# Spreading the reciprocals of later chunks by 32-row matmuls in a four-layer attention and MLP kernel

## The chip, the cores and the metric

The kernel runs on one core of a Trainium2 chip. The metric is the device time of one execution in microseconds. A core has five engines with a queue each: TensorE (PE) multiplies matrices, VectorE (DVE), ScalarE (ACT) and GpSimd (POOL) work element by element, and SyncE (SP) starts most DMAs. Matmuls write to PSUM, which has eight banks of 512 f32 columns by 128 partitions; ACT and DVE read them from there.

## The reference

The input is 2048 rows of 576 bf16 values. Four layers follow each other: attention (A), MLP (B), and both again with the same weights. The two layers, cut to what matters:

```python
def A(x):                       # x is already layer-normalized; 32 heads of 18
    q, k, v = split(x @ wqkv)
    pq, pk = phi(q), phi(k)     # phi(t) = (t + 1 if t > 0 else exp(t)) + 1e-6
    kv = einsum("bhsd,bhse->bhde", pk, v)
    z = einsum("bhsd->bhd", pk)
    num = einsum("bhqd,bhde->bhqe", pq, kv)
    den = einsum("bhqd,bhd->bhq", pq, z) + 1e-6
    return (num / den[..., None]) @ wo
def B(x):                       # x is layer-normalized, and once more in here
    return gelu(layernorm(x) @ w1 + b1) @ w2 + b2
x = x + A(layernorm(x)); x = x + B(layernorm(x))    # twice
```

## The kernel before

Rows are held in 16 blocks of 128 tokens; four blocks make a chunk of 512. The 32 heads lie in five groups (g): four of seven heads (126 rows) and one of four heads (72 rows). PE's instructions stand in the order in which the code writes them (each is chained to the one before). On the other engines a scheduler orders the instructions, and the code adds edges ("after=...") that keep one behind another on the same engine; such an edge is an order and no wait.

An attention layer first computes keys, values and most query maps, sums keys by values (kvT), and multiplies that into the output weights (kv_wo, L733; kvwo is its result). Then, by chunk:

- q_proj (L584) makes a query map of a group: five matmuls of 512 columns into a bank of ps_h, then phi by ACT (exp, L466, and identity, L467) and DVE (min and max) into pq. Some are left for this part of the layer: in layer 0 the last three, in layer 2 the last one; they are taken in the loop over blocks.
- den_stage (L748): 20 matmuls, with the array split into four tiles of 32 columns, give the denominators of a chunk as a 128 x 128 tile: partition 32j + h holds head h, and the columns are the tokens of block j. ACT takes the reciprocal by a logarithm and an exp (rden, one buffer).
- quad_stage (L767): DVE lays rden out as 128 x 512, zero outside its own quarter (quad_rden).
- scale_stage (L777): for a group, one matmul of 512 columns with a 0/1 matrix (head_bc) spreads the reciprocals over the rows of the group's heads; ACT copies the bank to SBUF (rden_bc), and DVE multiplies pq by it.
- wo_stage (L789): for a block, ten matmuls (five groups, two halves) accumulate the output in accA or accB in turn; DVE adds the residual row (L517), and SP stores the sum.

PSUM has two pools: ps_h, four banks of one kind that all of q_proj, den_stage, scale_stage and the transposes share, and accA and accB, of two banks each, for outputs, kv_wo and the few tiles written with a pair tag.

The entry (L802 to L829) does the steps of chunk 0 and the denominators of chunk 1. The loop over blocks (L830 to L849) then runs wo_stage for block t, takes a query map if one is left, and spreads the next chunk's reciprocals in its first two blocks, for three groups and then two; den_stage of the chunk after that follows in the second.

The sums of blocks 0 to 3 are also normalized for the MLP. LNPipe (L301) moves each through steps, one per tick: statistics (DVE by bn_stats, L351, or ACT by two passes with an accumulator, L333 and L342), the inverse root, the norm on POOL (L391), five transposes on PE (L423) and a copy by ACT. hold is the number of ticks before the statistics; the loop gives two ticks for each block up to 9, and one for the others. tp_at is the block behind which the transposes may go. In layer 0 the sums go to row buffers of a pool of nine, which a block keeps until it is normalized and stored; in layer 2 they overwrite the residual's own buffer.

The tile `turned` holds rows that DVE transposes for later chunks in the MLP layers.

Of the kernel before, what the change touches and what calls it, by code (L numbers as in the profile page):

```python
# [15 lines left out]
P = 128  # L16
# [12 lines left out]
CA = 512  # L29
# [5 lines left out]
def build(tc, A_x, A_wqkv, A_wo, B_w1, B_b1, B_w2, B_b2, out, dbg=None, n_layers=4):  # L35
    nc = tc.nc
    dbg = dbg or {}
    with ExitStack() as ctx:
# [420 lines left out]

        def phi_from_psum(ps_ap, out_ap, rows, n, turned_cols=False, after=None, dve_after=None, ident_after=None):  # L460
            e = work.tile([P, 512], BF16, name="phi_e", bufs=3)
            a = work.tile([P, 512], BF16, name="phi_a", bufs=2)
            e_out, a_out = e[0:rows, 0:n], a[0:rows, 0:n]
            if turned_cols:
                e_out, a_out, ps_ap = spread(e_out), spread(a_out), gather(ps_ap)
            exp = nc.scalar.activation(out=e_out, in_=ps_ap, func=ACT.Exp)  # L466
            ident_pass = nc.scalar.activation(out=a_out, in_=ps_ap, func=ACT.Identity, bias=C1, scale=1.0)  # L467
            if after is not None:
                for step in (exp, ident_pass):
                    tc.add_manual_dep(step.ins, after, NOSYNC, reason="broadcasts first")  # L470
            if ident_after is not None:
                tc.add_manual_dep(ident_pass.ins, ident_after, NOSYNC, reason="first rows first")
# [54 lines left out]
        def layer_A(li, next_kind, pre_a1=None):  # L527
# [56 lines left out]
            def q_proj(g, c, defer=False):  # L584
# [6 lines left out]
                if g == 0:  # L591
                    nc.gpsimd.memset(pq[(g, c)][96:P, 0:CA], 1.0)
                phi = lambda after=None, dve_after=None: phi_from_psum(qp[0:GR[g], :], pq[(g, c)][0:GR[g], 0:CA], GR[g], CA,
                                                       turned_cols=(li > 0), after=after, dve_after=dve_after)
                if defer:
# [137 lines left out]
            def kv_wo(g):  # L733
# [5 lines left out]
                out = kvwo[g][0:GR[g], :].rearrange("p (h n) -> p h n", h=2)  # L739
                if g % 2 or g == 4:  # L740
                    nc.vector.tensor_copy(out=out, in_=wp[0:GR[g], :, 0:HALF])
# [3 lines left out]
            quad_rden = {}  # L745
            rden_of = {}

            def den_stage(c, after=None, pair=None):  # L748
# [16 lines left out]
                rden_of[c] = rden  # L765

            def quad_stage(c, after=None):  # L767
# [8 lines left out]

            def scale_stage(g, c, pair=None):  # L777
                if pair:
                    bp = ps_acc.tile([P, 2, 512], F32, name="rden_pair", tag=pair)[:, 0, :]
                else:  # L780
                    bp = ps_h.tile([P, 512], F32, name="rden_ps", tag="h")
                pe(nc.tensor.matmul(bp[:, 0:CA], lhsT=head_bc[:, g, :], rhs=quad_rden[c][:, 0:CA], start=True, stop=True))  # L782
                rb = blk.tile([P, D], BF16, name="rden_bc", tag="blk")
                act_last["copy"] = nc.scalar.copy(out=rb[0:GR[g], 0:CA], in_=bp[0:GR[g], :]).ins.name
                mult = nc.vector.tensor_tensor(out=pq[(g, c)][0:GR[g], 0:CA], in0=pq[(g, c)][0:GR[g], 0:CA],  # L785
                                               in1=rb[0:GR[g], 0:CA], op=ALU.mult)
                dve_last["mult"] = mult.ins.name

            def wo_stage(t):  # L789
# [8 lines left out]
                if xn is not None and next_kind == "B" and t < TPC:  # L798
                    lnp.feed(xn, t, "B", "pool", "act", hold=(2, 4, 6, 8)[t], tp_at=6 + 2 * t,
                             **(dict(after="sum") if t % 2 else dict(stats="act", after="rden")))  # L800

# [9 lines left out]
            quad_stage(0)  # L811
            phi(after=act_last["rden"], dve_after=dve_last["quad"])
            if li > 0:
# [10 lines left out]
            late.append(q_proj(*q_left.pop(0), defer=True))  # L824
            scale_stage(4, 0)
            den_stage(1, after=act_last["copy"], pair="accB")
# [3 lines left out]
            for t in range(NT):  # L830
# [256 lines left out]
```

## Time and profile before

| | |
|---|---|
| Median of 3 runs | 766.45 us (766.34 to 767.07) |
| Profiled execution | 767.19 us, of which the span from first to last instruction 765.4 |
| Granted TensorE clock | 1.00 throughout |
| PE, busy | 759.5 us, 6522 matmuls |
| ACT, DVE, POOL, busy | 336.9, 271.8, 123.4 us |
| Layer 0, entry (70.7 to 77.7 us) | PE 6.81 of 7.00 us busy |
| Layer 0, loop over blocks (77.7 to 107.0) | PE 28.78 of 29.30, ACT 21.38, DVE 22.91 |
| Layer 2, entry (447.9 to 453.8) | PE 5.90 of 5.90 |
| Layer 2, loop over blocks (453.8 to 480.4) | PE 26.46 of 26.60, ACT 19.29, DVE 22.06 |

Times in the profile are microseconds from the first instruction. PEld is the loading of matmul weights, which runs beside the matmuls. A row of the timeline merges instructions of one line that follow each other, and where its engine sat idle before it, it names the releaser. Busy PE time counts overlapping matmuls as one stretch, with ends that are modelled, so a wait of PE is best read from the starts of successive rows.

### The profile page before, as it was taken

To read this page: it belongs to the slowest core of one execution; us is meant where nothing else is said; L and a number is where in the kernel's file an instruction comes from. 1 tells how busy PE (TensorE), PEld (TensorE's weight loads), DVE (VectorE), ACT (ScalarE), POOL (GpSimd) and SP (SyncE) were. 2 spreads that over 40 slices of the span, in tenths; PEclk is the share of its full clock that TensorE was granted. 3 is DMA by queue.
4 is the path that set the end of the run, shared out by engine and by line. 5 is a ranking of instruction groups with operands and counts; after the bars stand their busy time and mean duration, and the time that the engine had idled before them with its cause. 6 is when DMAs were issued, how large, how long until landed. Compare 5 with 4: busy or idle time off the path is not lost.

```text
span 765.4 us, 15654 instructions
## 1 busy us (share of the span) xinstructions
PE 759.5 (99%) x6522; PEld 492.3 (64%) x6522; DVE 271.8 (36%) x685; ACT 336.9 (44%) x752; POOL 123.4 (16%) x198
## 2 busy tenths in 40 slices
PE   8999999999999999999999999999999999999998
PEld 5776664675477457646777767447745764674476
DVE  7786864035113603400455678600240032000000
ACT  5888856304710660174057577560065036205600
POOL 4681322012100301200110004200020021001000
DMA  9992483016401631330246007530141033011000
GB/s 259 269 301 48 140 283 75 25 57 166 121 24 63 188 76 40 95 88 1 66 128 216 1 16 233 218 81 17 56 110 42 16 125 81 9 32 55 2 9 24
DMA packets 80289, 73.82 MB, mean 96 GB/s; under 512 B 36698, under 2 KB 64858, under 8 KB 80218
## 3 DMA queue, kind: packets, MB, share of 16 engines
q1 hardware_dynamic: 80218, 72.82, 32.4%
q8 instruction: 51, 0.84, 0.5%
q14 instruction: 20, 0.16, 0.1%
HBM read 48.03 MB, written 24.77 MB: 95 GB/s over the span
## 4 chain that ended last, share of the span: by engine, by line
PE 97%; ACT 1%; DVE 1%; DMA 1%; POOL 0%; issue 0%; SPq 0%; DVEq 0%
PE m_ps L968 36%; PE h_ps L910 20%; PE hp_ps L910 16%; PE q_ps L587 5%; PE wo_ps L794 4%; PE k_ps L539 3%; PE k_ps L610 3%; PE k_ps L627 2%; PE v_ps L560 1%; PE m_half L968 1%; PE v_ps L557 1%; PE tp L423 1%; PE rden_ps L782 1%; DMA wqkv_sb<-in_A_wqkv_dram 1%; PE kvacc L581 1%; PE k_tail L627 1%
## 5 line engine op out<-in xcount | busy, mean ns | idle before, releaser
L968 PE MATMUL m_ps<-w_sb,hT 128*128 128x288 bf16 x2232 | 274.8, 286 | 0.0
L968 PEld LDWEIGHTS <-hT 128*128 128x128 bf16 x2304 | 224.8, 98 | 59.8 <-issue 3.4
L910 PEld LDWEIGHTS <-w_sb 64*128 64x128 bf16 x2304 | 124.5, 94 | 136.5 <-issue 1.9
L910 PE MATMUL hp_ps<-yT,w_sb 64*128 64x512 bf16 x1152 | 178.0, 376 | 0.0
L910 PE MATMUL h_ps<-yT,w_sb 64*128 64x512 bf16 x1152 | 148.0, 376 | 0.0
L915 ACT COPY relay_sb<-relay_sb 128x1 f32<-128x1 f32 x144 | 28.6, 198 | 262.3 <-PE h_ps L910 220.0
L906 ACT ACTIVATE hT<-h_ps,b1T 128x512 bf16<-128x512 f32 x144 | 91.2, 684 | 44.4 <-PE h_ps L910 43.7
L374 POOL TENSOR_TENSOR ln_rstd<-ln_u,neg_half 128x1 f32<-128x1 f32 x64 | 36.7, 575 | 375.0 <-DVE ln_u L365 226.8
L906 ACT ACTIVATE hT<-hp_ps,b1T 128x512 bf16<-128x512 f32 x144 | 91.2, 693 | 0.0
L517 DVE TENSOR_TENSOR xbf<-m_ps,xo 128x576 bf16<-128x576 f32 x15 | 11.4, 758 | 212.8 <-PE m_ps L968 212.8
L517 DVE TENSOR_TENSOR xo<-m_ps,xo 128x576 f32<-128x576 f32 x16 | 12.1, 758 | 174.5 <-PE m_ps L968 174.5
L500 POOL TENSOR_TENSOR xo<-xo,b_bc 128x576 f32<-128x576 f32 x32 | 40.9, 1282 | 98.8 <-DMA xo<-x_d 59.8
L910 PE MATMUL h_ps<-yT,w_tail 64*128 64x512 bf16 x144 | 54.1, 376 | 0.0
L910 PE MATMUL hp_ps<-yT,w_tail 64*128 64x512 bf16 x144 | 54.1, 376 | 0.0
L587 PE MATMUL q_ps<-yT,wqkv_sb 128*126 128x512 bf16 (+1 forms) x200 | 49.8, 380 | 0.0
L794 PE MATMUL wo_ps<-kvwo,pq 126*128 126x288 bf16 (+1 forms) x320 | 43.4, 286 | 0.7 <-DVE xn L517 0.4
L910 PEld LDWEIGHTS <-w_tail 64*128 64x128 bf16 x288 | 27.1, 94 | 17.1
L794 PEld LDWEIGHTS <-pq 126*128 126x128 bf16 (+1 forms) x320 | 30.1, 97 | 10.9 <-DVE pq L785 0.9
L466 ACT ACTIVATE phi_e<-k_ps 128x288 bf16<-128x288 f32 x46 | 19.3, 419 | 39.0 <-PE k_ps L610 36.0
L474 DVE TENSOR_SCALAR phi_e<-phi_e 128x288 bf16<-128x288 bf16 (+2 forms) x86 | 25.1, 291 | 20.6 <-ACT phi_e L466 20.0
L587 PEld LDWEIGHTS <-wqkv_sb 128*126 128x126 bf16 (+1 forms) x200 | 24.9, 131 | 11.7 <-issue 0.4
L466 ACT ACTIVATE phi_e<-q_ps 126x512 bf16<-126x512 f32 (+1 forms) x40 | 23.8, 596 | 17.5 <-PE q_ps L587 17.3
(135 smaller groups left out, 659.1 us busy)
## 6 DMA issues: line engine op xcount, KB each, us to landing
xo<-x_d SPq DMA_DIRECT2D x48, 288.0 KB
x_d<-xo SPq DMA_DIRECT2D x32, 288.0 KB
xl<-x_d SPq DMA_DIRECT2D x24, 288.0 KB
y_d<-turned SPq DMA_DIRECT2D x40, 144.0 KB
w_sb<-in_B_w_dram SPq DMA_DIRECT2D x6, 864.0 KB
yT<-y_d SPq DMA_DIRECT2D x10, 512.0 KB
w_sb<-in_B_w_dram SPq DMA_DIRECT2D x9, 512.0 KB
x_d<-xn SPq DMA_DIRECT2D x16, 288.0 KB
```

The source lines that it names most:

```text
L374: nc.gpsimd.tensor_tensor(out=rstd[:], in0=it["u"][:], in1=neg_half[:], op=ALU.pow)
L466: exp = nc.scalar.activation(out=e_out, in_=ps_ap, func=ACT.Exp)
L474: low = nc.vector.tensor_scalar(out=e[0:rows, 0:n], in0=e[0:rows, 0:n], scalar1=1.0, scalar2=1e-6, op0=ALU.min, op1=ALU.add)
L500: nc.gpsimd.tensor_tensor(out=xo[:], in0=xo[:], in1=b2_bc[:], op=ALU.add)
L517: total = nc.vector.tensor_tensor(out=xn[:, cols].rearrange("p (h n) -> p h n", h=2), in0=halves, in1=xo[:, cols].rearrange("p (h n) -> p ...
L539: pe(nc.tensor.matmul(kp[:, 0:HALF], lhsT=yT[:, k, tok], rhs=wqkv_sb[:, k, D + half * HALF: D + (half + 1) * HALF], start=(k == 0), stop=( ...
L587: pe(nc.tensor.matmul(qp[0:GR[g], :], lhsT=wqkv_sb[:, k, GO[g]:GO[g] + GR[g]], rhs=yT[:, k, c * CA:(c + 1) * CA], start=(k == 0), stop=(k ...
L794: pe(nc.tensor.matmul(wp[:, half, 0:HALF], lhsT=pq[(g, c)][0:GR[g], j * P:(j + 1) * P], rhs=kvwo[g][0:GR[g], half * HALF:(half + 1) * HALF ...
L906: act_last["gelu"] = nc.scalar.activation(out=to, in_=ps, func=ACT.Gelu_apprx_tanh, bias=b1T[:, f:f + 1], scale=1.0).ins.name
L910: mm = pe(nc.tensor.matmul(dst[n], lhsT=wt, rhs=mv, start=(seen[n] == 0), stop=(seen[n] == 8)))
L915: relay = nc.scalar.copy(out=relay_sb[:, 1:2], in_=relay_sb[:, 0:1])
L968: pe(nc.tensor.matmul(acc[half][:, 0:HALF], lhsT=hT[f][:, j * P:(j + 1) * P], rhs=w2_sb[:, f, half * HALF:(half + 1) * HALF], start=(f == ...
```

## The change

It changes seven things in the attention layers:

1. For chunks 1 to 3 and groups 0 to 3, quarter_stage replaces the four matmuls of 512 columns by 16 of 128 columns, from 32 rows each: quarter i of the array takes rows 32i to 32i + 31 of rden and of head_bc and writes bank i of four ps_h banks. ACT copies the four banks to `turned`, now used as a place for them, and quarter_scale multiplies group by group from there. Group 4 and chunk 0 keep the old way.
2. These steps have new places. Chunk 1: quarters after block 1, multiplies after block 2. Chunks 2 and 3: quarters after the last block of the chunk two before, multiplies after the first two blocks of the chunk before, two groups each.
3. den_stage of chunk 2 goes from block 1 to block 2; that of chunk 3 stays at block 5 (with quad_stage right behind it in the order of the code).
4. The query maps left in layer 0 go after blocks 0 and 2 (one, then two) instead of 0, 1 and 2; in layer 2 the one left stays after block 0.
5. Statistics of blocks 0 and 2 go to DVE and those of blocks 1 and 3 to ACT (before, the other way round); hold is (2, 8, 8, 10) in layer 0 and (2, 2, 2, 4) in layer 2 instead of (2, 4, 6, 8).
6. In the entry, group 4 of chunk 0 is multiplied straight from PSUM (direct), without ACT's copy.
7. In layer 0's entry, kv_wo(3) is copied by ACT instead of DVE, and the exp of the first query map there need no longer follow the reciprocal.

```diff
             if after is not None:
-                for step in (exp, ident_pass):
+                for step in (ident_pass,) if exp_first else (exp, ident_pass):
                     tc.add_manual_dep(step.ins, after, NOSYNC, reason="broadcasts first")
...
-                if g % 2 or g == 4:
+                if g in (1, 4) or g == 3 and li > 0:
                     nc.vector.tensor_copy(out=out, in_=wp[0:GR[g], :, 0:HALF])
...
-            def scale_stage(g, c, pair=None):
+            def scale_stage(g, c, pair=None, direct=False):
...
-                rb = blk.tile([P, D], BF16, name="rden_bc", tag="blk")
-                act_last["copy"] = nc.scalar.copy(out=rb[0:GR[g], 0:CA], in_=bp[0:GR[g], :]).ins.name
+                spread_rows = bp
+                if not direct:
+                    spread_rows = blk.tile([P, D], BF16, name="rden_bc", tag="blk")
+                    act_last["copy"] = nc.scalar.copy(out=spread_rows[0:GR[g], 0:CA], in_=bp[0:GR[g], :]).ins.name
...
+            def quarter_stage(c):
+
+                rden = rden_now["tile"]
+                banks = [ps_h.tile([P, 512], F32, name="rden_ps", tag="h") for _ in range(4)]
+                for g in range(4):
+                    for i in range(4):
+                        rows = slice(32 * i, 32 * (i + 1))
+                        pe(nc.tensor.matmul(banks[i][0:126, g * P:(g + 1) * P], lhsT=head_bc[rows, g, 0:126],
+                                            rhs=rden[rows, :], start=True, stop=True))
+                spread_rows = turned[:].rearrange("p a t c -> p (a t c)").rearrange("p (i w) -> p i w", i=4)
+                for i in range(4):
+                    act_last["copy"] = nc.scalar.copy(out=spread_rows[0:126, i, 0:4 * P], in_=banks[i][0:126, :]).ins.name
+
+            def quarter_scale(c, groups, after):
+                spread_rows = turned[:].rearrange("p a t c -> p (a t c)").rearrange("p (i w) -> p i w", i=4)
+                for g in groups:
+                    scaled = pq[(g, c)][0:126, 0:CA].rearrange("p (i n) -> p i n", i=4)
+                    mult = nc.vector.tensor_tensor(out=scaled, in0=scaled,
+                                                   in1=spread_rows[0:126, :, g * P:(g + 1) * P], op=ALU.mult)
+                    tc.add_manual_dep(mult.ins, after, NOSYNC, reason="sums first")
+                    dve_last["mult"] = mult.ins.name
...
-                    lnp.feed(xn, t, "B", "pool", "act", hold=(2, 4, 6, 8)[t], tp_at=6 + 2 * t,
-                             **(dict(after="sum") if t % 2 else dict(stats="act", after="rden")))
+                    lnp.feed(xn, t, "B", "pool", "act", hold=(2, 2, 2, 4)[t] if li > 0 else (2, 8, 8, 10)[t], tp_at=6 + 2 * t,
+                             **(dict(after="sum") if t % 2 == 0 else dict(stats="act", after="rden")))
...
-            phi(after=act_last["rden"], dve_after=dve_last["quad"])
+            phi(after=act_last["rden"], dve_after=dve_last["quad"], exp_first=(li == 0))
...
-            scale_stage(4, 0)
+            scale_stage(4, 0, direct=True)
...
                 wo_stage(t)
-                for late in list(rden_of):
-                    quad_stage(late, after=dve_last["sum"])
-                if q_left:
+                total = dve_last["sum"]
+                if c + 1 < NCA:
+                    for g in ((), (), (0, 1, 2, 3), ())[j] if c == 0 else ((0, 1), (2, 3), (), ())[j]:
+                        quarter_scale(c + 1, (g,), after=total)
+                    if t == 1:
+                        quarter_stage(1)
+                    if j == 3 and c + 2 < NCA:
+                        quarter_stage(c + 2)
+                    if j == (2 if c == 0 else 0):
+                        scale_stage(4, c + 1)
+                if j == (2 if c == 0 else 1) and c + 2 < NCA:
+                    den_stage(c + 2)
+                    if c > 0:
+                        quad_stage(c + 2, after=total)
+                if t == 3:
+                    quad_stage(2, after=total)
+                if q_left and t in (0, 2):
                     q_proj(*q_left.pop(0))
-                if c + 1 < NCA:
-                    for g in ((0, 1, 2), (3, 4), (), ())[j]:
-                        scale_stage(g, c + 1)
-                if j == 1 and c + 2 < NCA:
-                    den_stage(c + 2)
+                    if t == 2:
+                        q_proj(*q_left.pop(0))
```

More of the change, by code (lines that the diff above doesn't have):

```diff
@@ L458, in phi_by_dve, with phi_from_psum @@
             dve_last["phi"] = top.ins.name
-        def phi_from_psum(ps_ap, out_ap, rows, n, turned_cols=False, after=None, dve_after=None, ident_after=None):
+        def phi_from_psum(ps_ap, out_ap, rows, n, turned_cols=False, after=None, dve_after=None, ident_after=None,
+                          exp_first=False):
             e = work.tile([P, 512], BF16, name="phi_e", bufs=3)
@@ L592, in q_proj @@
                     nc.gpsimd.memset(pq[(g, c)][96:P, 0:CA], 1.0)
-                phi = lambda after=None, dve_after=None: phi_from_psum(qp[0:GR[g], :], pq[(g, c)][0:GR[g], 0:CA], GR[g], CA,
-                                                       turned_cols=(li > 0), after=after, dve_after=dve_after)
+                phi = lambda after=None, dve_after=None, exp_first=False: phi_from_psum(qp[0:GR[g], :], pq[(g, c)][0:GR[g], 0:CA], GR[g], CA,
+                                                       turned_cols=(li > 0), after=after, dve_after=dve_after,
+                                                       exp_first=exp_first)
                 if defer:
@@ L746, in layer_A @@
             rden_of = {}
+            rden_now = {}
             def den_stage(c, after=None, pair=None):
@@ L765, in den_stage @@
                 rden_of[c] = rden
+                rden_now["tile"] = rden
             def quad_stage(c, after=None):
@@ L782, in scale_stage @@
                 pe(nc.tensor.matmul(bp[:, 0:CA], lhsT=head_bc[:, g, :], rhs=quad_rden[c][:, 0:CA], start=True, stop=True))
-                rb = blk.tile([P, D], BF16, name="rden_bc", tag="blk")
-                act_last["copy"] = nc.scalar.copy(out=rb[0:GR[g], 0:CA], in_=bp[0:GR[g], :]).ins.name
+                spread_rows = bp
+                if not direct:
+                    spread_rows = blk.tile([P, D], BF16, name="rden_bc", tag="blk")
+                    act_last["copy"] = nc.scalar.copy(out=spread_rows[0:GR[g], 0:CA], in_=bp[0:GR[g], :]).ins.name
                 mult = nc.vector.tensor_tensor(out=pq[(g, c)][0:GR[g], 0:CA], in0=pq[(g, c)][0:GR[g], 0:CA],
-                                               in1=rb[0:GR[g], 0:CA], op=ALU.mult)
+                                               in1=spread_rows[0:GR[g], 0:CA], op=ALU.mult)
                 dve_last["mult"] = mult.ins.name
+            def quarter_stage(c):
[17 more added lines that the diff above has]
+                    dve_last["mult"] = mult.ins.name
             def wo_stage(t):
```

## The prediction, made before the change was run

> **What bounds the kernel now.** I read the page's busy times and its chain of waits first, to see which engine a saving has to reach.
>
> ```profile
> PE 759.5 (99%) x6522; PEld 492.3 (64%) x6522; DVE 271.8 (36%) x685; ACT 336.9 (44%) x752; POOL 123.4 (16%) x198
> PE 97%; ACT 1%; DVE 1%; DMA 1%; POOL 0%; issue 0%; SPq 0%; DVEq 0%
> ```
>
> TensorE (PE) is the bound: only fewer or shorter PE steps, or fewer PE waits, can shorten the run. Busy time is no measure of that, since pipelined matmuls overlap in it; what counts is the time from one step's start to the next one's. So I read PE's rows of the timeline in the two attention layers, where the change sits: columns are start, length, engine, line, operation, count, then the idle time with what ended it.
>
> ```profile
> 75.12 0.41 PE L736 MATMUL kvwo_ps<-wo_sb,kvT 72*72 72x288 bf16 x2
> 75.72 0.38 PE L782 MATMUL rden_pair<-quad_rden,head_bc 128*128 128x512 bf16 x1 [0.19 <-DVE kvwo L741]
> ...
> 77.01 0.38 PE L782 MATMUL rden_ps<-quad_rden,head_bc 128*128 128x512 bf16 x1
> 77.32 0.47 PE L756 MATMUL den_pair<-pq,zsel 127*32 127x128 bf16 x20
> 77.72 1.71 PE L794 MATMUL wo_ps<-kvwo,pq 126*128 126x288 bf16 x10
> 79.27 1.24 PE L587 MATMUL q_ps<-yT,wqkv_sb 128*126 128x512 bf16 x5
> ...
> 89.03 0.81 PE L782 MATMUL rden_ps<-quad_rden,head_bc 128*128 128x512 bf16 x3
> 89.68 1.40 PE L794 MATMUL wo_ps<-kvwo,pq 126*128 126x288 bf16 x10
> ...
> 93.36 1.40 PE L794 MATMUL wo_ps<-kvwo,pq 126*128 126x288 bf16 x10
> 95.14 1.39 PE L794 MATMUL wo_ps<-kvwo,pq 126*128 126x288 bf16 x10 [0.38 <-DVE xn L517]
> ...
> 448.37 0.96 PE L647 MATMUL kv_ps<-k,wqkv_sb 128*126 128x126 bf16 x15
> 449.16 1.27 PE L587 MATMUL q_ps<-yT,wqkv_sb 128*126 128x512 bf16 x5
> ```
>
> A spreading matmul of 512 columns (L782) costs (89.68 - 89.03) / 3 = 0.216 us. A block of output matmuls (L794) costs 1.23 where nothing waits. PE's losses are then few. Layer 0: 0.35 before rden_pair (two kvwo steps of 0.12 end at 75.37), 0.32 in the first output block (1.55 for 1.23), 0.55 before the block at 95.14 (the one before it ends at 94.59). Layer 2, in the same view: 0.32 in its first output block (453.77 to 455.33) and 0.12 before its rden_pair. Together 1.66 us.
>
> The last two views say who causes these and what the nearest operations cost (groups: busy in all, mean ns of one).
>
> ```profile
> 94.33 0.76 DVE L517 TENSOR_TENSOR xn<-wo_ps,xo_pair 128x576 f32<-128x576 f32 x1 [1.09 <-POOL y_ring L391]
> ```
>
> ```profile
> L968 PEld LDWEIGHTS <-hT 128*128 128x128 bf16 x2304 | 224.8, 98 | 59.8 <-issue 3.4
> L910 PEld LDWEIGHTS <-w_sb 64*128 64x128 bf16 x2304 | 124.5, 94 | 136.5 <-issue 1.9
> L784 ACT CAST rden_bc<-rden_ps 126x512 bf16<-126x512 f32 (+1 forms) x38 | 20.0, 596 | 6.4 <-PE rden_ps L782 6.3
> L785 DVE TENSOR_TENSOR pq<-pq,rden_bc 126x512 bf16<-126x512 bf16 (+1 forms) x40 | 16.3, 436 | 1.0 <-ACT rden_bc L784 0.5
> L456 DVE SCALAR_TENSOR_TENSOR pk<-k_ps,phi_e 128x288 bf16<-128x288 f32 x18 | 8.2, 456 | 0.6
> ```
>
> **Quarters, six times (chunks 1 to 3 of two layers).** Removed: 4 x 0.216 = 0.864 us of PE. Added: 16 matmuls of 128 columns from 32 rows, in four groups of four, and two changes of the array's division. No row shows this form. The nearest is the denominator step (L756): five groups of four 32-column tiles and both changes, from 77.01 + 0.216 = 77.23 to 77.72, or 0.49 us. Without a fifth group (0.057) that is 0.43. From above: every load and matmul in turn, 16 x 0.053 (L647, 126-column weights: 0.79 / 15) and about 0.19 for the changes, 1.04; unhidden loads are a rival below. I take 0.43, because 64-row weight loads (L910) do overlap: 2304 x 94 ns is 217 us and covers only 124.5, where 2304 x 98 at L968 covers 224.8. Saving 0.43 each, **-2.6 us**; bounds -2.6 and +1.1 (0.18 x 6).
>
> TensorEngine Tiling (Array Packing) of the Trainium skill, in Key Properties, says that tiles load and multiply in parallel and that a change of tiling mode drains the array. The denominator rows agree on the drain: 77.01 to 77.32 is 0.31 for a 0.216 step.
>
> ScalarE (ACT) copies four banks of 0.6 us as before, DVE multiplies four times as before, with the same types; the strided second input I price at nothing (quad_rden, strided too, also steps at 0.34). At 0.69, the price of a pass from PSUM, a chunk's four would take 1.4 us longer on DVE; two to three output blocks of 1.23 cover that, and without them it would all be PE's wait.
>
> **The four banks.** A quarter stage needs all four ps_h banks before its first four matmuls; before, each matmul needed one. So PE waits in it, with the next output block queued behind, until ACT has emptied every bank handed out before. I laid the loop out by hand with the steps above and ACT's pace of 0.48 a pass. Layer 0, chunk 1: the three query maps end at about 81.0 and PE arrives at 81.06: 0.1. Chunk 2: a slack of 0.4. Chunk 3: the first transposed block's copy ends 0.2 late. Layer 2 now has its statistics on ACT (1.57 us, two passes of 0.8) between chunk 2's reciprocal and its four copies, so the fifth spreading matmul finds no bank for 0.35; chunks 1 and 3 wait 0.1 each. In layer 0 the transposes of blocks 1 and 3 meet a normalization about 0.15 late each. Together **+1.15**; bounds 0 and +2.6, at which the quarters earn nothing.
>
> **Entry, layer 0.** kv_wo(3) goes from DVE to ACT, which empties its bank at about 75.0 (ACT's passes from 73.0 on, with one more kvwo of 0.52 and an exp of 0.48 already done ahead of the log). The wait of 0.35 at rden_pair goes, and the last spreading matmul runs at 76.66. Its multiply reads PSUM: 288 columns cost 456 ns (L456), 576 cost 758 (L517), so 512 cost about 0.69 in place of a 0.59 copy and a 0.43 multiply. The multiply ahead of it is late next (ACT's fourth copy ends at 77.06), so it runs from 77.44 to 78.13, and the first output block's fifth matmul goes at 78.2 in place of 78.64: **-0.44**, bounds -0.67 (both waits gone) and +0.26 (the longer multiply with nothing won). The earlier exp moves the log by 0.04; the query matmuls until 74.45 hide that (quad_rden ends near 74.1), and without them it would cost those 0.04.
>
> **Entry, layer 2.** Only the direct multiply changes: 453.65 to 454.33, the fifth matmul at 454.4 in place of 454.56: **-0.16**, bounds -0.32 and +0.26.
>
> **Row buffers, layer 0.** The 0.55 before 95.14 is a residual sum that waits for a row buffer until POOL has normalized the second block (1.09 idle). Now block 0 gets DVE statistics early and frees its buffer some 4 us sooner, so a free one should be at hand: **-0.55**, bounds -0.55 and +1.4 (second rival). The query steps keep their number; queries that move from blocks 0 to 2 into blocks 0 and 2 cost nothing in steps, and their banks are counted above. No DMA is added, and SP's stores go out with the sums as before; POOL does the same norms.
>
> **Sum.** -2.6 + 1.15 - 0.44 - 0.16 - 0.55 = -2.6 us. The profiled execution took 767.19 (span 765.4 and 1.79 around it), 0.74 above the median; it would take 764.6. From the median of 766.45: **763.9**.
>
> **Rivals.** *Banks give it back.* Where ACT's last pass ahead of a quarter ends 0.43 us or more after PE arrives, that quarter earns nothing. For it: 0.1 to 0.2 of slack in my layout, and any statistics pass (0.8) placed in front decides. Against it: in the busy times by stage ACT works 21.4 of the 29.3 us from 77.7 to 107.0. All six lost: another 1.45 us of waits, 765.3 to 766, centre 765.7.
>
> *Layer 0's row buffers again.* Block 1's statistics now follow the third denominators on ACT (about 90.9), 1.57 on ACT and 2.2 on POOL, so its buffer is free at 94.7. If a sum that is ready at 91.6 gets that buffer, PE, with 1.7 us of other work, waits 1.4; and the 0.55 stays: 765.9.
>
> *Weight loads in turn (slower).* Place: the 16 loads of 126 columns. What a quarter replaces is won or lost at (0.864 - 0.19) / 16 = 42 ns a pair. At 53 ns (L647 in steady state) each loses 0.18 and the total is 767.5; at 105 ns each (L647's first step, where the load isn't hidden: the second matmul starts 105 ns after the first) 16 x 0.105 + 0.19 is 1.87, a loss of 1.0, and the total 772.5. For it: L756's 32-column loads are so short that overlap there proves little. Against it: L910's overlap, though with only two row tiles. TensorE: Matmul & The Clock Gate of the Trainium skill, LDWEIGHTS (loading the stationary operand), says that a load takes its columns / 1.2 ns whatever its rows, so 32 rows load no faster than 128; by that rule in turn 16 loads would be 1.68 us. The steady 53 ns at L647 is half of the rule's 105.
>
> **How the numbers follow.** 0.2%, 1.5 us, is about what a measurement of this kernel can tell from no change, so faster ends at 764.9 and slower begins at 768.0. Forecast 0.60, with its own range of 762.3 to 764.9 (below, all new waits absent and each gain at its bound; above, 1.0 more of waits): faster. Banks 0.12 and row buffers 0.08: within. Loads in turn 0.20: 0.04 at the short price (within), 0.16 above 768. Hence 0.60, 0.24, 0.16, and a range of 762.3 to 768.0 that leaves out the long-price loads and a little below.
>
> **What would show it.** In the profile after, 96 matmuls of 32 rows, groups of four some 55 ns apart, and 0.43 us from the output block before a quarter to the one after it. A pace of 53 ns for each matmul, or 1 us for a stage, proves the loads rival. A PE row of the quarter or of the spreading matmul that waits on ACT's copies, statistics or query maps proves the banks; a sum in layer 0 that waits on POOL, the buffers. The first output block of layer 0 should take about 1.5 us from its own start, with rden_pair no longer waiting on DVE. I am wrong most simply if a layout by hand that leaves 0.1 us of slack is off by 1 us in several places.

## The result and the profile after

The changed kernel takes 774.06 us (median of 6 runs, 772.16 to 775.22), the kernel before 766.95 in the same runs; the ratio is 1.0090, with an interval of 1.0079 to 1.0101. It is slower by 7.1 us where 2.6 less had been forecast. The profiled execution took 774.04 us, its span 772.3, at a granted clock of 0.995.

On the page of the changed kernel, the busy times and the chain of waits that answer to those of before:

```profile
PE 760.1 (98%) x6594; PEld 491.7 (64%) x6594; DVE 271.8 (35%) x684; ACT 336.6 (44%) x751; POOL 124.7 (16%) x198
PE 93%; DVE 2%; DMA 2%; ACT 1%; POOL 1%; issue 1%; SPq 0%; DVEq 0%; ACTq 0%; POOLq 0%
```

PE's busy time hardly moves, but PE's part of the chain falls from 97 to 93%, and DMA's and POOL's rise. The new time is waiting, and it ends on transfers and on normalizations. To place it, I took the starts of PE's rows at the seams of the stages: the first z_ps matmul of a layer (sums of the keys) opens the entry, its first wo_ps matmul the loop over blocks, and the next layer's first h_ps matmul ends it. In us, of the profiled executions:

| kernel | start to entry 0 | entry 0 | loop 0 | layer 1 and 2's start | entry 2 | loop 2 | layer 3 to end | span |
|---|---|---|---|---|---|---|---|---|
| before | 70.40 | 7.32 | 29.30 | 339.42 | 7.33 | 26.60 | 285.03 | 765.40 |
| after | 70.03 | 7.07 | 30.18 | 339.42 | 7.33 | 32.74 | 285.56 | 772.33 |
| difference | -0.37 | -0.25 | +0.88 | 0 | 0 | +6.15 | +0.53 | +6.93 |

The first column moves by some tenths among kernels that do not differ there (69.7 to 70.4 in the runs below). Nearly all of the loss is in the loop over blocks of layer 2; the 0.53 behind it is its consequence, and layer 0's loop is longer too.

**Layer 0.** PE's rows of the timeline after (start, length, operation, count, idle time and what ended it):

```profile
77.10 0.66 PE L822 MATMUL wo_ps<-kvwo,pq 126*128 126x288 bf16 x4
78.04 0.91 PE L822 MATMUL wo_ps<-kvwo,pq 72*128 72x288 bf16 x6 [0.28 <-DVE pq L791]
78.79 1.24 PE L588 MATMUL q_ps<-yT,wqkv_sb 128*126 128x512 bf16 x5
79.87 1.40 PE L822 MATMUL wo_ps<-kvwo,pq 126*128 126x288 bf16 x10
81.20 0.45 PE L802 MATMUL rden_ps<-rden,head_bc 32*126 32x128 bf16 x16
81.58 1.41 PE L822 MATMUL wo_ps<-kvwo,pq 126*128 126x288 bf16 x10
...
95.10 0.38 PE L786 MATMUL rden_ps<-quad_rden,head_bc 128*128 128x512 bf16 x1
96.07 0.40 PE L423 MATMUL tp<-ident,y_ring 128*128 128x128 bf16 x4 [0.60 <-POOL y_ring L391]
96.95 0.23 PE L423 MATMUL tp<-ident,y_ring 128*128 128x128 bf16 x1 [0.48 <-POOL y_ring L401]
97.02 2.63 PE L822 MATMUL wo_ps<-kvwo,pq 126*128 126x288 bf16 x20
...
99.76 2.63 PE L822 MATMUL wo_ps<-kvwo,pq 126*128 126x288 bf16 x20
103.11 0.53 PE L423 MATMUL tp<-ident,y_ring 128*128 128x128 bf16 x5 [0.72 <-POOL y_ring L391]
```

The output block at 79.87 would end its steps at 81.10; the quarters start at 81.20 and the next block at 81.58. A stage of 16 matmuls so takes 0.48 us from block to block, where the four old ones took 0.86. But the transposes now wait for POOL: 0.76 at 96.07 (the spreading matmul at 95.10 ends its step at 95.31), 0.67 within those five (0.95 for 0.28), and 0.89 at 103.11 (99.76 and two blocks of 1.23 is 102.22). That is 2.3 us, and three quarters save 1.2. ACT's rows show why block 3 is late:

```profile
97.80 0.69 ACT L333 ACTIVATE ln_dump<-xn 128x576 bf16<-128x576 f32 x1
...
98.60 1.28 ACT L448 ACT_TABLE_LOAD   x1
...
100.00 0.76 ACT L342 ACTIVATE ln_dump<-xn,ln_mv 128x576 bf16<-128x576 f32 x1
```

The load of ACT's table for the MLP, 1.28 us, falls between the two statistics passes of that block. In *stats_alone* below, where no transpose waits, it stands at 100.93, behind both passes.

**Layer 2.** PE's rows at the end of the loop, and DVE's residual sums there:

```profile
476.55 1.40 PE L822 MATMUL wo_ps<-kvwo,pq 126*128 126x288 bf16 x10
479.77 1.39 PE L822 MATMUL wo_ps<-kvwo,pq 126*128 126x288 bf16 x10 [1.82 <-DVE xo L518]
484.29 2.56 PE L822 MATMUL wo_ps<-kvwo,pq 126*128 126x288 bf16 x10 [3.13 <-DVE xo L518]
486.77 1.57 PE L949 MATMUL h_ps<-yT,w_sb 64*128 64x512 bf16 x8
```

```profile
478.96 0.76 DVE L518 TENSOR_TENSOR xo<-wo_ps,xo 128x576 f32<-128x576 f32 x1 [2.90 <-DMA xo<-x_d]
483.48 1.49 DVE L518 TENSOR_TENSOR xo<-wo_ps,xo 128x576 f32<-128x576 f32 x2 [3.76 <-DMA xo<-x_d]
```

Three output blocks that took 3.8 us before take 10.2. The row of before is

```profile
476.58 3.86 PE L794 MATMUL wo_ps<-kvwo,pq 126*128 126x288 bf16 x30
```

and its next row starts at 480.37. In the changed kernel PE waits for a bank that a sum must empty, and the sum waits for its residual row to be loaded (DMA xo<-x_d). The last block then runs at half speed (2.5 us from start to start for 1.23). Why the rows are late stands in SP's rows of the timeline; L496 loads a residual row, L525 stores a sum:

```profile
465.95 3.66 SPq L496 DMA_DIRECT2D xo<-x_d  x2
469.71 0.85 SPq L525 DMA_DIRECT2D x_d<-xo  x2
475.77 0.32 SPq L496 DMA_DIRECT2D xo<-x_d  x1
476.20 0.84 SPq L525 DMA_DIRECT2D x_d<-xo  x2
477.14 1.30 SPq L496 DMA_DIRECT2D xo<-x_d  x2
```

and in the chain of waits from 455 to 490 us, where two transfers are the longest pieces (start, length, what):

```profile
469.71 6.04 DMA x_d<-xo
...
477.14 6.21 DMA xo<-x_d
```

Nine row buffers hold the residual rows, and a sum overwrites its row; so row 9 and those after it are loaded into a buffer that is free again. A buffer is free when its sum is stored and, for blocks 0 to 3, normalized too. SP takes its DMAs in the order of its queue. In the changed kernel that order is (L a load, S a store, by block): L9 S2 S3 L10 L11 S4 S5 L12 S6 S7 L13 L14 S8 L15. The two DMAs merged at 465.95 are L10 and L11; L11 waits until 469.29 for block 2's buffer, which POOL's norm (L391, 467.45 to 469.27) frees; that norm took 1.82 us, where those of blocks 1 and 3 take 0.82, and why stays open. S4, whose sum was done at 465.5, stands behind it until 469.71 and lands 6.04 us later; L12 needs its buffer and leaves at 475.77; S6 and S7, both long summed, stand behind L12; L13 leaves at 477.14, needs 6.21 us, and the last sums wait for it. SP's waits for that stretch say the same (in all, times, longest; the last row is L11's):

```profile
SPq L496 <- DMA x_d<-xo: 6.6, 3, 5.2
SPq L496 <- POOL y_ring L391: 4.7, 2, 3.3
SPq L496 <- POOL y_ring L401: 2.4, 1, 2.4
```

In the kernel before the order is L9 S3 S4 L10 S5 L11 S6 L12 S7 L13 S8 L14. Its rows from S3 to L11, and the waits of its loads:

```profile
464.85 1.28 SPq L524 DMA_DIRECT2D x_d<-xo  x2
467.30 0.32 SPq L495 DMA_DIRECT2D xo<-x_d  x1
467.71 0.41 SPq L524 DMA_DIRECT2D x_d<-xo  x1
468.77 0.32 SPq L495 DMA_DIRECT2D xo<-x_d  x1
```

```profile
SPq L495 <- DMA x_d<-xo: 3.1, 3, 1.5
SPq L495 <- POOL y_ring L391: 2.3, 1, 2.3
SPq L495 <- POOL y_ring L401: 1.4, 1, 1.4
```

S4, the second of the first row, leaves at 465.75, and a load waits for a store 3.1 us in all, 1.5 at most.

### The profile page after: what moved, and what is told of

It is laid out like the page before. It is cut to its first block, busy times and chain, and to the rows that moved or that the text cites. A ratio compares the mean times of both kernels' runs of the same rounds, so it can differ in the third digit from the quotient of the medians.

```text
span 772.3 us, 15791 instructions
## 1 busy us (share of the span) xinstructions
PE 760.1 (98%) x6594; PEld 491.7 (64%) x6594; DVE 271.8 (35%) x684; ACT 336.6 (44%) x751; POOL 124.7 (16%) x198
## 4 chain that ended last, share of the span: by engine, by line
PE 93%; DVE 2%; DMA 2%; ACT 1%; POOL 1%; issue 1%; SPq 0%; DVEq 0%; ACTq 0%; POOLq 0%
PE m_ps L1007 36%; PE h_ps L949 20%; PE hp_ps L949 16%; PE q_ps L588 5%; PE k_ps L540 3%; PE k_ps L612 3%; PE wo_ps L822 2%; PE k_ps L629 2%; PE v_ps L561 1%; PE m_half L1007 1%; PE v_ps L558 1%; DMA xo<-x_d 1%; PE tp L423 1%; DMA x_d<-xo 1%; DVE xo L518 1%; DVE pq L791 1%
## 5 line engine op out<-in xcount | busy, mean ns | idle before, releaser
L374 POOL TENSOR_TENSOR ln_rstd<-ln_u,neg_half 128x1 f32<-128x1 f32 x64 | 36.1, 566 | 415.7 <-DVE ln_u L365 224.7
L822 PE MATMUL wo_ps<-kvwo,pq 126*128 126x288 bf16 (+1 forms) x320 | 45.4, 291 | 5.7 <-DVE xo L518 5.2
```

The source lines that it names most:

```text
L374: nc.gpsimd.tensor_tensor(out=rstd[:], in0=it["u"][:], in1=neg_half[:], op=ALU.pow)
L822: pe(nc.tensor.matmul(wp[:, half, 0:HALF], lhsT=pq[(g, c)][0:GR[g], j * P:(j + 1) * P], rhs=kvwo[g][0:GR[g], half * HALF:(half + 1) * HALF ...
```

## The experiments

The theory after this reading: the quarters do what was forecast, and the loss is SP's queue in layer 2, where stores with finished sums stand behind loads that wait for row buffers; layer 0's loss is the new places of the statistics. Rivals: the slow transfers themselves, whatever their order; the new statistics alone; the quarters' own steps.

**Stores ahead of loads (stores_first).** The changed kernel with

```diff
...
+                if t >= 9:
+                    tc.add_manual_dep(load.ins, store_of[(li, t - 6)], NOSYNC, reason="stores go first")
...
```

> The changed kernel with one order added on SyncE's queue in layer 2: the load of residual row t (9 and later) stands behind the store of block t - 6. Every engine keeps its work, the statistics stay where the change put them, and row 11 still gets block 2's buffer and still waits for POOL to normalize it. Theory 1 (SyncE's queue: the load of row 11 waits for that buffer, the stores of blocks 4 and 5 stand behind it, and every later load waits for a buffer whose store went out late): the two waits of 2.1 and 3.4 us before the last output blocks and the halved clock behind them go; the loop of layer 2 takes 25.5 us instead of 32.7, the first MLP group 0.87 instead of 1.41, and the time is 766.3 (765.8 to 767.0). Theory 2 (the normalization on POOL is simply too late for row 11's buffer, whatever the order): row 11 still lands late and at least half of the loss stays, 770 or more. Theory 3 (the quarters or the slower DMAs in that stretch): no change, 774.

Measured: 767.29 us (766.84 to 767.67), ratio to before 1.0004 with its interval [0.9995, 1.0013]; layer 2's loop 26.31. The order of one queue, which costs no instruction, accounts for 6.8 of the 7.1 us lost. The total is 1 us over the expectation, since the loop ends at 26.3 and not at 25.5: the quarters' saving there is not won yet.

**One swap (one_load_late).** The same edge for row 11 alone (`if t == 11:`).

> The changed kernel with one swap in SP's order in layer 2: the load of residual row 11, which waits for the third block's normalization, goes behind the stores of rows 4 and 5 instead of ahead of them. Theory (those two stores held behind that load, twice over since rows 12 and 13 take their buffers, are the loss): the stores leave about 3 us earlier, at 466.5 instead of 469.7 and 470.1, row 12 is loaded from about 470 instead of 475.8, row 13 from about 471.5 instead of 477.1; layer 2's loop takes 27 to 28.5 us instead of 32.7, the total 768.0 to 769.5 instead of 774.0, and PE's steps of 240 ns behind the loop are gone. Rival (the transfers themselves are slow there, whatever the order): the store of row 4 still takes 6 us and the loop stays above 31, the total above 772.5.

Measured: 767.43 us (767.00 to 767.78), 1.0006 [0.9997, 1.0015]; loop 26.32. SP's rows of this kernel:

```profile
466.65 1.55 SPq L528 DMA_DIRECT2D x_d<-xo  x2
469.58 0.94 SPq L497 DMA_DIRECT2D xo<-x_d  x2
470.62 2.89 SPq L528 DMA_DIRECT2D x_d<-xo  x2
473.60 0.96 SPq L497 DMA_DIRECT2D xo<-x_d  x2
```

S4 leaves at 466.65, L12 at 470.2 as the second of the two merged at 469.58, L13 at 473.6: 3.1, 5.6 and 3.5 us earlier than in the changed kernel. The last three blocks take 3.8 us again (476.84 to 480.64). More came back than expected, all that *stores_first* brought: the load of row 11 ahead of two stores is the cause of the 6 us, by the two rounds that follow from it. That transfers are slow whatever the order is refuted.

**The same order in the kernel before (bad_order, forced_order).** First only stores 4, 5 and 6 behind load 11:

```diff
...
+                if t == 11:
+                    for late in (4, 5, 6):
+                        tc.add_manual_dep(store_of[(li, late)], load.ins.name, NOSYNC, reason="stores go last")
...
```

> The kernel before, with nothing of the change, but with one order on SyncE's queue in layer 2: the stores of blocks 4, 5 and 6 stand behind the load of residual row 11. Row 11 then gets block 2's buffer and waits for POOL to normalize it, as in the changed kernel. No engine's work differs. Theory 1 (SyncE's queue): the stores leave about 5 us late and bunched, rows 13 to 15, whose buffers they free, land late, and PE waits before the last output blocks: the loop of layer 2 takes 30 to 32 us instead of 26.6, and the time is 770 to 772.5. Rivals (the quarters, or the places of the statistics, are the cause by their load on ScalarE, VectorE or POOL): 767, as before.

Measured: 767.81 us, 1.0015 [1.0006, 1.0024]; loop 27.53, so +0.9. The direction is right, the size missed: here row 12 took block 3's buffer, which POOL frees, so no second load waited for a late store. Then the whole order was forced to that of the changed kernel:

```diff
+        ORDER = "L8 S0 S1 L9 S2 S3 L10 L11 S4 S5 L12 S6 S7 L13 L14 S8 L15 S9".split()
...
+                for first, then in zip(ORDER, ORDER[1:]):
+                    tc.add_manual_dep(row_dma[then], row_dma[first].name, NOSYNC, reason="rows in this order")
```

> The kernel before with SP's order of loads and stores in layer 2 forced to be that of the changed kernel; the scheduler then gives row 12 the fourth block's buffer and rows 13 and 14 those of rows 4 and 5, where the changed kernel gives 12 and 13 to those. Theory (the order alone costs, also with the old spreading and the old statistics): stores 4 and 5 leave behind load 11, at about 470, layer 2's loop grows by 1 to 3.5 us to 27.6 to 30.1, the total is 767.8 to 770.3. Rival (the order costs only where the quarters have brought PE forward): the loop stays within 0.5 us of 26.6 and the total is 766.5 to 767.3.

Measured: 770.75 us (768.82 to 771.21), 1.0044 [1.0031, 1.0057]; loop 29.76, so +3.2, and 0.83 more behind it. PE's rows of its timeline:

```profile
476.60 2.63 PE L807 MATMUL wo_ps<-kvwo,pq 126*128 126x288 bf16 x20
481.46 2.17 PE L807 MATMUL wo_ps<-kvwo,pq 126*128 126x288 bf16 x10 [2.23 <-DVE xo L530]
```

So the order costs with the old spreading and the old statistics too. It gives half of the 6.15, with one wait in place of two, and that wait comes about another way: row 12's load waits until 473.43 for POOL's norm of block 3, row 13's leaves behind it at 474.74 without waiting for a store, and lands 5.79 us later. The buffers differ, as expected; that they make the whole of the rest is not shown, since no run forces both the order and the buffers.

**The statistics (stats_alone, l2_stats_old, stats_old).** First the kernel before with the changed kernel's statistics and nothing else:

```diff
-                    lnp.feed(xn, t, "B", "pool", "act", hold=(2, 4, 6, 8)[t], tp_at=6 + 2 * t,
-                             **(dict(after="sum") if t % 2 else dict(stats="act", after="rden")))
+                    lnp.feed(xn, t, "B", "pool", "act", hold=(2, 2, 2, 4)[t] if li > 0 else (2, 8, 8, 10)[t], tp_at=6 + 2 * t,
+                             **(dict(after="sum") if t % 2 == 0 else dict(stats="act", after="rden")))
```

> The kernel before with the new statistics alone (hold and engines of both layers), no quarters and the old entry. Theory 1: in layer 2 the stores of blocks 4 and 5 now stand ahead of the load of row 11, so the loss doesn't appear there: loop of layer 2 within 1 us of 26.6. Layer 0: blocks 1 and 3 are normalized late by their own hold, whatever the quarters: PE waits before their transposes, so 1 to 2 us more in layer 0's loop. 767.5 to 769. Rival (the statistics as such cause layer 2's loss): 772 or more.

Measured: 766.94 us, 1.0002 [0.9993, 1.0011]; loops 29.06 and 26.95. Alone they cost nothing in the total: layer 2's loop is 0.35 longer, within the 1 us expected, but layer 0's is 0.24 shorter, where 1 to 2 more had been expected, a miss. Then the changed kernel with the old statistics, in layer 2 only and in both layers (the diff above, turned round):

> The changed kernel with layer 2's statistics as they were before (hold 2, 4, 6, 8; blocks 0 and 2 on ScalarE, 1 and 3 on VectorE); layer 0 keeps the new ones, and quarters and entry stay. The order of the loads then lets row 11 take block 4's buffer instead of block 2's. Theory 1: the loss of layer 2 goes as in the run with stores first, 766.3 (765.8 to 767.0). Theory 3 (quarters): 773 to 774.

Measured: 769.26 us, 1.0027 [1.0015, 1.0038]; loop 2 at 28.43. A miss: better than after by 4.3 in the loop, but not down to the expected total. Row 10's load now waits for block 1's normalization until 469.1, with S5 behind it.

> The changed kernel with the statistics of both layers as before; quarters, their places and the entry stay. Theory 1 with a second cause in layer 0 (block 1's and block 3's statistics are so late on ScalarE that PE waits before their transposes, 2.3 us in all by the trace): another 1.5 us below the run with layer 2's statistics undone, since the wait for a row buffer (0.55) comes back: 764.7 (764.2 to 765.4), faster than before. If the quarters were the cause in layer 0, no lower than 766.

Measured: 767.41 us, 1.0010 [1.0001, 1.0019]; loop 0 at 28.57, 1.6 less than after, and no transpose of layer 0 waits; loop 2 at 28.13. Layer 0's loop fell as expected, though the wait of 0.55 for a row buffer did not come back; the total missed by layer 2's part. So layer 0's loss comes from new statistics and quarters together: each alone gives a loop under 29.1, both 30.18.

**The quarters alone (quarters_alone).** The kernel before with points 1 to 4 of the change: the quarters and the places of the steps.

```diff
-                    for g in ((0, 1, 2), (3, 4), (), ())[j]:
-                        scale_stage(g, c + 1)
...
+                        quarter_scale(c + 1, (g,), after=total)
...
+                        quarter_stage(c + 2)
...
+                        scale_stage(4, c + 1)
...
```

> The kernel before with the quarters and the places of their steps, of the denominators and of the query maps alone: statistics and entry as before. By the trace a quarter stage takes 0.47 us with both changes of the array's division, against 0.864 removed: six times 0.39 is 2.3 us, less waits for banks of 0.5 or so. 765.0 (764.4 to 765.8), and 0.25 above the run with both statistics undone, which is what the entry gave by the trace (5.04 us against 5.29 in layer 0, nothing in layer 2). A rival: the entry gives its 0.6 as forecast, and the two runs differ by that.

Measured: 767.92 us, 1.0010 [1.0001, 1.0019]; loop 0 at 28.43, 0.87 shorter, loop 2 at 27.63, 1.0 longer. A miss for the same reason: row 10's load waits for block 1's buffer until 468.19, and a later load 3.4 us for a store. In layer 0, which has no such loads, the loop gets shorter; in layer 2 the shorter PE only meets the rows earlier. Layer 2's loss, too, thus comes from statistics and quarters together: alone they add 0.35 and 1.0 to its loop, together 6.15.

**Both mended (stats_old_stores_first, l0_old_stores_first).** The changed kernel with stores first, and with the old statistics in both layers, or in layer 0 alone:

> The changed kernel with the statistics of both layers as before, and layer 2's loads behind the stores. Without that order the run took 767.4, with 28.1 us in layer 2's loop, since row 10's load waits for POOL with block 5's store behind it. Theory 1: row 10's load is the same, and block 5's store still follows it here, so little changes: layer 2's loop 27.5 to 28.1, 767.0 to 767.4. If the order alone decides and not the time of the normalization, 26.3 and 765.6.

Measured: 767.09 us, 1.0006 [0.9997, 1.0015]; loops 28.52 and 28.16, as expected. The order is not enough either: block 1's late normalization still frees its buffer late (row 10's load leaves at 467.67).

```diff
...
+                if t >= 9:
+                    tc.add_manual_dep(load.ins, store_of[(li, t - 6)], NOSYNC, reason="stores go first")
...
-                    lnp.feed(xn, t, "B", "pool", "act", hold=(2, 2, 2, 4)[t] if li > 0 else (2, 8, 8, 10)[t], tp_at=6 + 2 * t,
-                             **(dict(after="sum") if t % 2 == 0 else dict(stats="act", after="rden")))
+                    lnp.feed(xn, t, "B", "pool", "act", hold=(2, 2, 2, 4)[t] if li > 0 else (2, 4, 6, 8)[t], tp_at=6 + 2 * t,
+                             **(dict(after="sum") if (t % 2 == 0) == (li > 0) else dict(stats="act", after="rden")))
```

> The changed kernel with layer 0's statistics as before and, in layer 2, the loads of rows 9 and later behind the stores of the blocks six before them. By the stages of the runs so far: layer 0's loop 28.6 us as in the run with both statistics undone (30.2 in the changed kernel), layer 2's loop 26.3 as in the run with stores first. The run with stores first took 767.3, so 765.7 (765.2 to 766.3), faster than before. If the two don't add (a buffer that one takes from the other), 767.

Measured: **765.44 us** (765.1 to 765.9), 0.9983 [0.9974, 0.9992], faster than both kernels (the kernel before took 766.69 in the same runs). Loops 28.52 and 26.31, entry 0 at 7.07. The view of PE's waits in layer 0's loop holds two of 0.3 us, for the direct multiply and for a bank copy, and none of a transpose.

So with the stores first the new statistics are right for layer 2, where they free row buffers early (loop 26.31, with the old ones 28.16), and wrong for layer 0.

**One row buffer fewer (eight_rows).** The kernel before with `bufs=8` in the pool of rows.

> The kernel before with eight row buffers instead of nine. Theory (the loop over blocks is near the pace of free buffer, load, sum, store): layer 2's loop takes 28 us or more instead of 26.6, with sums waiting for loaded rows, and layer 0's sums wait longer for a free buffer (loop 29.8 or more instead of 29.3); total 768.5 to 771. Rival (a buffer to spare): both loops within 0.3 us of before, total 766.5 to 767.2.

Measured: 767.47 us (766.84 to 768.39), 1.0008 [0.9999, 1.0017]; loop 2 at 28.04, 1.4 longer as expected, but loop 0 at 28.89, 0.4 shorter, and the total is under the 768.5 to 771 expected. The loops are those of an execution of 768.28 us, one of the longer ones. The ninth buffer is in use in layer 2. In layer 0 the 0.55 wait for a row buffer is gone with fewer buffers, so it did not lie in their number; that it lay in which buffer a sum was handed fits this, but no run shows it.

## Why the prediction was wrong

**The step that failed** is the last of the part on row buffers: "No DMA is added, and SP's stores go out with the sums as before". No DMA is added, but their order in SP's queue changed, and with it when the stores leave. The prediction costed row buffers in layer 0 alone, where sums go to fresh buffers. In layer 2 a later residual row needs a buffer that an earlier block must have stored and normalized, and both hang on things that the change moved: the statistics, and the place of the sums among PE's steps. That term was costed at nothing without naming what covers it. It measured +6.15 in the loop and +0.53 behind it; one swap of SP's order removes it (one_load_late). None of the three rivals was this one; the second had a sum wait for a row buffer, but in layer 0. The evidence was at hand: in the trace of before, SP's loads in layer 2 already wait, 3.1 us for stores and 3.7 for POOL (the rows above), and no part of the prediction shows those rows.

**Quarters: right.** -0.43 each was forecast, -0.39 measured (0.864 less 0.47 to 0.48 in the six stages, from the end of the block before, 81.10 above, to the next one, 81.58). The view of this tile and line in the changed kernel holds the 96 matmuls of 32 rows (duration in ns, smallest, median, largest; first and last start; form):

```profile
L802 PE MATMUL rden_ps<-rden,head_bc x96: 216/216/264, 81.2 to 469.2; 32*126 32x128 bf16 x96
```

Within a stage the four matmuls of a group start 3 to 4 ns apart; the second group starts 106 ns after the first, the others 57 ns apart. So the four row tiles load and multiply side by side, as the nearest row (the denominators) had said. The stage takes 0.38 from its first start to the next block's, with 0.10 ahead of it. The rival of loads in turn is refuted: all 16 start within 0.23 us, where 16 steps of 57 ns alone are 0.92. (The forecast's 53 ns at L647 is a mean over ten steps with weights of 126 columns, at 57 ns, and five of 72 columns, at 32 to 35; with 57 its sum from above is 1.11 in place of 1.04.) By the rule of the Trainium skill (TensorE: Matmul & The Clock Gate, LDWEIGHTS) 16 loads in turn would be 1.68, an estimate from its figure; the other page's rule, that tiles load and multiply in parallel (the Trainium skill, TensorEngine Tiling (Array Packing), Key Properties), is the one that the trace bears out.

**The four banks: partly.** In layer 2 the fifth spreading matmul of chunk 2 waits 0.37 (the block at 462.08 ends its steps at 463.31, the matmul runs at 463.68), for 0.35 forecast. The other chunks wait 0.1 or less ahead of a stage. But a sum on DVE stands behind three multiplies, one of them 0.81 long instead of 0.41, and PE waits 0.46 for it before the block at 467.62. The multiplies had been costed as before, and the other passes from `turned` in that loop take 0.41 to 0.54; why the one at 465.38 takes 0.81 stays open.

**The transposes of layer 0, mis-sized:** 0.15 late each in the sum, 2.3 us measured for the two. For block 1 the forecast had 1.57 us on ACT; the trace after has 2.54, from 91.27 to 93.81, since the copy of block 0's transposes (92.35) falls between the two passes, and on POOL a step of block 2 (L374, 95.98) stands ahead of the copy of block 1's last columns (L401). For block 3 the layout did not count the four bank copies (2.05 us in one row) ahead of its statistics, nor the table load. That the old statistics remove it is shown (stats_old, loop 1.6 shorter); how much of it is the table load was not tried by itself.

**Entry, layer 0: the wait went, the gain didn't.** Forecast -0.44 at the fifth matmul of the first output block; the entry is 0.25 shorter, and the block then takes 1.69 to the query map instead of 1.55, so -0.11. rden_pair no longer waits for DVE, as forecast. DVE's rows show what took its place:

```profile
75.64 0.75 DVE L743 CAST kvwo<-kvwo_ps 72x576 bf16<-72x576 f32 x1
76.31 1.08 DVE L791 TENSOR_TENSOR pq<-pq,rden_bc 126x512 bf16<-126x512 bf16 x3
77.31 0.68 DVE L791 TENSOR_TENSOR pq<-pq,rden_ps 72x512 bf16<-72x512 bf16 x1
```

The trace after runs 0.37 us ahead by its first column, so the forecast's times are 0.37 earlier in it. ACT's fourth copy ends at 76.71, as laid out (77.06 less 0.37 is 76.69). But DVE comes from the copy of kvwo with three multiplies in a row, and the direct one starts at 77.31, not at 77.07: 0.24 of the gain is lost on DVE's own queue. The multiply itself takes 0.68, for 0.69 forecast. Another 0.12 was never there: the fifth matmul of before starts at 78.52, where the forecast had 78.64.

**Entry, layer 2:** +0.05 instead of -0.16; its entry stays at 7.33, and the first output block takes 1.60 instead of 1.55. The reason is the same: DVE runs three multiplies from 453.14, and the direct one starts at 454.14 and not at 453.91 (the forecast's 453.65 and the 0.26 by which this trace is later there).

**Row buffers, layer 0:** PE's wait of 0.55 is gone, as forecast, but the forecast's reason, block 0's early statistics, isn't shown. The wait is gone as well in *quarters_alone* and *stats_old*, where those statistics stand as before, and in *eight_rows*. The size was right, then, and the reason stays open. One residual sum in the changed kernel still waits for POOL (DVE, until 98.51), without holding PE.

Summed, with the terms as measured: -0.39 x 6, -0.11, +0.05, -0.55, +2.3 for the transposes, +0.83 for the two waits in layer 2, which is +0.2. What is left of the +6.9, about 7.1 with the 0.37 that the part ahead of the entry was shorter, is SP's queue: two waits of 2.0 and 3.3, and 1.25 and 0.53 for the steps at half speed behind them. Without it, *stores_first* stands level with the kernel before, and not at the 763.9 that was forecast.

## What to carry to other kernels

When a change moves work in a loop that loads into recycled buffers, write out the DMA queue's order for both kernels, with what each entry waits for: a finished store behind a load that waits for a buffer holds back the next load that needs the store's buffer, and a few such pairs cost more than any step that the change shortens. Read the waits of the DMA queues before costing a move at nothing; waits that end just in time in the profile of before are slack that a faster engine uses up (quarters_alone). And a good placement in one layer need not be good in the next: here, with the stores first, the new places of the statistics save 1.85 us of layer 2's loop (28.16 to 26.31) and cost 1.65 in layer 0's (28.52 to 30.17).

## What the runs showed of the hardware

A store of 288 KB landed in 6.04 us, though in the last 2.55 of them little was moving. The two parts of that stretch (length; PE, PEld, DVE, ACT, POOL busy; clock, DMA share, GB/s):

```profile
469.70:473.20 3.50, 3.50 (x33) 2.75 (x31) 2.64 (x6) 3.49 (x7) 2.09 (x5) 1.00 0.75 240
473.20:475.75 2.55, 2.55 (x25) 2.08 (x24) 2.01 (x5) 1.49 (x3) 0.00 (x0) 1.00 0.07 22
```

L11, S4 and S5, 885 thousand bytes together, were under way; 840 thousand had moved by 473.2 (240 GB/s by 3.5 us), and the last 2.55 us moved 56 thousand, a sixteenth of the 885, at a share of 0.07, about one of 16 engines. That fits one DMA engine late with its part, and a store that counts as landed with the last part; the rows don't name the engines, so this is argued and not shown. In one_load_late the same store landed in 3.6 us at most (466.65 until the load that waits for its buffer, at 470.2). Why the last sixteenth was late stays open, and so does what the 6 us of this store add to the loss by themselves.

A wait of PE can cost after it has ended. Behind waits of 2.0 and 3.3 us the last block of layer 2 and the first MLP matmuls stepped at half speed (2.5 us for 1.23; 1.41 for 0.87), and the run's mean granted clock fell to 0.995. When it fell is read from the clock in two stretches, with the columns as above:

```profile
479.77:481.07 1.30, 1.30 (x10) 0.97 (x10) 0.00 (x0) 0.00 (x0) 0.00 (x0) 1.00 1.14 193
481.07:484.29 3.22, 0.09 (x2) 0.00 (x1) 0.81 (x2) 0.00 (x0) 0.00 (x0) 0.50 0.95 355
```

The block behind the first wait ran at full speed, and the clock was halved at its end, 1.3 us after that wait was over and before the second one; it came back at 487.9. In forced_order a single wait of 2.4 us ended at 481.46, and the clock fell from 1.00 to 0.50 at 481.90, within the block behind it, which took 2.1 us for 1.23. The Trainium skill (TensorE: Matmul & The Clock Gate, Part 1: The HAM clock gate) has the clock halved after an idle window of about 3.4 us. Here it fell behind single waits of 2.0 and 2.4 us, so in these runs a shorter wait was enough.
